# One core, a fused attention, mixture-of-experts and FFN kernel: transposes of the pooled attention's exponentials go behind the next tile's q and k transposes in each step

## The chip, the cores and the metric

The kernel runs on one core of a Trainium2 chip. The metric is the device time of one execution in microseconds (us), lower is better. The engines are named as in the profile: PE (TensorE's matmuls), PEld (its weight loads), DVE (VectorE), ACT (ScalarE), POOL (GpSimd) and SP (SyncE, which here issues nearly all DMAs).

## What is computed

Three layers in a row. The first adds two attentions over q, k, v of shape 4 x 8 x 576 x 64: one over q, k, v pooled by four rows, its output repeated four times, and one local, with a mask of three rows to each side. The second sends each of the 2304 tokens through the one of eight experts that its gate picks. The third is a dense FFN with softplus.

```python
def _attn_ref(q, k, v):                       # factor = 4
    q_d = q.reshape(B, H, Sd, factor, D).mean(axis=3)      # k_d, v_d likewise
    out_d = sm_attn(q_d, k_d, v_d)
    out_up = np.repeat(out_d, factor, axis=2)
    mask = np.abs(pos[:, None] - pos[None, :]) < factor
    scores = np.where(mask, scale * np.matmul(q, k.transpose(0, 1, 3, 2)), -1e9)
    ...
    return out_up + np.matmul(attn, v)

def _moe_ref(x, modality_id, w_gate, modality_bias, w1, w2):
    logits = x @ w_gate + modality_bias[modality_id]
    e_idx = np.argmax(logits, axis=1)
    ...
    out[mask] = gate_w[mask, None] * (np.maximum(x[mask] @ w1[e], 0.0) @ w2[e])

def _moe2_ref(x, w_in, w_out):
    h = x @ w_in
    return (np.maximum(h, 0.0) + np.log1p(np.exp(-np.abs(h)))) @ w_out
```

## The kernel before

The program has two parts. `phase_a` computes the attention and the gate for 18 tiles of 128 tokens (four batches of 4.5 tiles) and writes them to DRAM; `phase_cd` gathers tokens by expert and runs the experts and the FFN. The first part takes roughly the first 205 us of the span, and the change lies in it.

`phase_a` is a software pipeline. A loop counts steps `t`, and each step calls the stages that the string `ORDER` names, from left to right (`ORDER` for steps 0 to 17, `TAIL0` and `TAIL` after that). Stages with nothing to do are skipped. Those that matter here:

- **LG** (`load_vg`, L662 to L666) loads v of a whole batch in four pieces through two buffers, `vg`; DVE adds four rows to one (`vh`, then `vd`). **LV** (`load_v`, L653) loads the v windows.
- **S** (`local_s`, L776 to L781) is tile t's local scores: 16 matmuls on PE into two PSUM banks, the mask added on DVE, the row maximum on DVE. **E** (`local_e`, L786, L787) subtracts it on POOL and exponentiates on ACT.
- **P** (`prep`, L674 to L695) takes a later tile (tile t+5 from step 2 on): four transposes of q and four of k on PE, each group into a bank of its own. ACT copies q out twice (`qbd`, L678), DVE sums four columns of q to one from the same bank (`qd`, L687), ACT copies k (`kT`, L690), and POOL sums k from SBUF (`h2`, `kd`, L693, L695). P ends with the loads of q and k of a tile three further on (L646).
- **DS** (`down_s`, L718 to L723) is one unit of the pooled attention (four heads of a batch): 12 score matmuls into two banks, maximum and subtraction on DVE, exponentials on ACT (`dp`, L723). **DT** (`down_t`, L733, L734) works in the step after on that unit: 12 transposes of the exponentials on PE into three banks, which ACT copies out (`dpt`). **DO** (`down_o`, L745 to L757) multiplies them with `vd`.
- **T** (`local_t`, L796, L797) transposes the local exponentials of tile t-1, **O** (`local_o`, L809 to L813) multiplies them with v. **M** and **G** are the gate, **X** transposes finished tiles for it, **U** and **LU** add the pooled output.

There are eight pooled units, two for each batch. DS runs in the steps in which one is waiting and DT one step later, so DT has work in steps 3, 4, 5, 6, 10, 11, 14 and 15. `PSL` lets P run ahead until the last tile is prepared in step 12. Both stages have work in steps 3, 4, 5, 6, 10 and 11.

All PSUM tiles of `phase_a` come from one tag of eight banks (`b1`). The text of the program doesn't fix the queues: the tile framework's planner puts each engine's instructions in order, with the place in the program as their priority and its own model of time for when they are ready, and it hands a bank to a new tile when a model's reader has released it. A tile that gets a bank waits on the chip for the readers of the tile that had it. Each engine then runs its queue strictly in that order.

```python
    elif what == "DT":
        for x in d_s:
            down_t(*x)
...
    elif what == "P":
        prep_to(PS(t))
```

Of the kernel before, what the change touches and what calls it, by code (L numbers as in the profile page):

```python
# [19 lines left out]
def tile_attention_moe_ffn(  # L20
# [16 lines left out]
    B, H, S, D = q.shape  # L37
# [548 lines left out]
    def phase_a(actx):  # L586
# [520 lines left out]
        LDA, LVA, OL, DN, UN = 2, 1, 1, 1, 2  # L1107
# [1 line left out]
        PSL = (3, 6, 7, 8, 9, 10, 11, 12, 13, 14, 15, 16, 17, 18, 19, 19, 21, 22)  # L1109
        TAIL0 = "DN Z LG LV S DT P E T DS DO U X O U M X M LU XT G G G W"  # L1110
        TAIL = "DN Z LG DS LV S DT P E T O DO LU U X M F G G F F G F W"
        ORDER = "DN Z LG LV S DT P M G T DS X U LU O E DO W"

        def PS(t):
            return PSL[t] if t < len(PSL) else t + 5
# [7 lines left out]
        while q_lu[0] < NTT or q_u or q_x or q_m or q_g:  # L1123
            t += 1
            for what in (ORDER if t < 18 else TAIL0 if t == 18 else TAIL).split():
                step(t, what)
# [262 lines left out]
    with ExitStack() as actx:  # L1389
        phase_a(actx)  # L1390
# [36 lines left out]
```

## Time and profile before

| | us |
|---|---|
| median of 3 runs | 922.46 (918.93 to 923.62) |
| the profiled execution | 925.12 |
| its span, first to last instruction | 923.4 |
| PE busy in the span | 853.3 (92%) |
| DVE busy | 654.7 (71%) |
| ACT busy | 547.1 (59%) |
| POOL busy | 214.8 (23%) |

A busy share is a mean over stages that are bound by different things, so a stage is read by itself: first the busy time and DMA share of a stretch, then the instructions in order of time. A row of the timeline begins with its start and its length in us; behind it, in brackets, stands how long its engine had been idle before it, and what ended that.

### The profile page before, as it was taken

How to read it: one execution, taken by the hardware profiler on the slowest of the kernel's cores; microseconds unless marked ns; L12 is line 12 of the kernel's file. 1: busy time of each engine (PE TensorE's matmuls, PEld its weight loads, DVE VectorE, ACT ScalarE, POOL GpSimd, SP SyncE). 2: the span in 40 equal slices, each digit the busy share in tenths (PEclk: the TensorE clock that was granted, in tenths of full speed). 3: DMA queues.
4: the chain of work that ended last, by engine and by line, in shares of the span. 5: the costliest groups of instructions: out<-in, count | busy, mean ns of one | idle time of the engine just before them, and what ended most of it. 6: DMA issues, size and time to landing. Idle time of an engine off the chain costs nothing. (4 is left out here: it accounts for less than half of the span.)

```text
span 923.4 us, 15325 instructions
## 1 busy us (share of the span) xinstructions
PE 853.3 (92%) x5356; PEld 725.9 (79%) x5356; DVE 654.7 (71%) x1271; ACT 547.1 (59%) x935; POOL 214.8 (23%) x263
## 2 busy tenths in 40 slices
PE   6797899868899999999999999899999999999996
PEld 6687788756777766786687898789899998999984
DVE  6576487678699988976857798656656665666662
ACT  3553564453699777876857677656545555455451
POOL 8322554230243342511001222202000000000001
PEclk9998899799999999999999999999999999999999
DMA  9999785672934599577354333202001001000000
GB/s 164 191 174 195 171 199 126 177 194 94 309 123 138 175 368 332 205 265 252 115 194 147 99 94 109 69 12 65 27 12 35 23 12 34 24 12 12 24 1 34
DMA packets 109112, 115.68 MB, mean 125 GB/s; under 512 B 68448, under 2 KB 83552, under 8 KB 109024
## 3 DMA queue, kind: packets, MB, share of 16 engines
q1 hardware_dynamic: 101072, 98.28, 38.0%
q0 software_dynamic: 4960, 16.28, 5.5%
q8 instruction: 44, 0.72, 0.3%
q10 hardware_dynamic: 2992, 0.04, 0.2%
q14 instruction: 44, 0.36, 0.1%
HBM read 92.93 MB, written 21.65 MB: 124 GB/s over the span
## 5 line engine op out<-in xcount | busy, mean ns | idle before, releaser
L333 DVE TENSOR_TENSOR wl<-raw,wh 128x1024 fp32r<-128x1024 f32 x152 | 187.6, 1256 | 34.8 <-ACT wh L332 31.8
L332 ACT ACTIVATE wh<-raw 128x1024 fp32r<-128x1024 f32 x152 | 159.2, 1064 | 39.8 <-DMA raw<-in_moe_w_dram 16.7
L552 PE MATMUL p<-yh,wh 128*128 128x384 f32 x384 | 131.6, 343 | 11.3 <-DVE e L1239 10.1
L556 PE MATMUL p<-yh,wl 128*128 128x384 f32 x384 | 129.4, 337 | 0.0
L555 PE MATMUL p<-yl,wh 128*128 128x384 f32 x384 | 129.3, 337 | 0.0
L552 PE MATMUL p<-wh,gh 128*128 128x512 f32 x288 | 113.8, 395 | 1.1 <-ACT gh L1244 1.1
L555 PE MATMUL p<-wl,gh 128*128 128x512 f32 x288 | 113.2, 393 | 0.0
L556 PE MATMUL p<-wh,gl 128*128 128x512 f32 x288 | 101.4, 395 | 0.1
L1238 ACT ACTIVATE u<-u 128x384 f32<-128x384 f32 x96 | 50.1, 524 | 80.1 <-DVE e L1237 80.1
L552 PEld LDWEIGHTS p<-yh,wh 128*128 128x128 f32 x384 | 72.1, 188 | 18.7 <-DVE e L1239 14.2
L1245 DVE TENSOR_TENSOR gl<-e,gh 128x384 fp32r<-128x384 f32 x96 | 57.5, 600 | 40.7 <-ACT gh L1244 39.9
L1244 ACT ACTIVATE gh<-e 128x384 fp32r<-128x384 f32 x96 | 50.1, 523 | 45.1 <-DVE e L1240 44.8
L555 PEld LDWEIGHTS p<-yl,wh 128*128 128x128 f32 x384 | 72.2, 188 | 3.0
L1231 ACT ACTIVATE e<-p 128x384 f32<-128x384 f32 x96 | 46.4, 488 | 46.3 <-PE p L556 42.8
L556 PEld LDWEIGHTS p<-yh,wl 128*128 128x128 f32 x384 | 72.1, 188 | 0.3
L1192 POOL DMA_INDIRECT yg<-ys,pos x18 | 19.1, 1060 | 216.4 <-PE p L1209 205.7
L1237 DVE SCALAR_TENSOR_TENSOR e<-u,e 128x384 f32<-128x384 f32 x96 | 55.2, 577 | 13.4 <-ACT u L1234 11.2
L556 PEld LDWEIGHTS p<-wh,gl 128*128 128x128 f32 x288 | 54.0, 188 | 12.9 <-DVE gl L1245 0.8
L552 PEld LDWEIGHTS p<-wh,gh 128*128 128x128 f32 x288 | 54.1, 188 | 10.5 <-ACT gh L1244 1.5
L1240 DVE TENSOR_TENSOR e<-e,u 128x384 f32<-128x384 f32 x96 | 55.3, 579 | 9.0 <-ACT u L1238 1.3
L555 PEld LDWEIGHTS p<-wl,gh 128*128 128x128 f32 x288 | 54.2, 188 | 8.7
L552 PE MATMUL p<-wh,hh 128*128 128x512 f32 x144 | 58.9, 409 | 1.8 <-ACT y L1170 1.5
(256 smaller groups left out, 1800.4 us busy)
## 6 DMA issues: line engine op xcount, KB each, us to landing
raw<-in_moe_w_dram SPq DMA_DIRECT2D x40, 512.0 KB
cv<-in_moe_w_in_dram SPq DMA_DIRECT2D x16, 512.0 KB
cv<-in_moe_w_out_dram SPq DMA_DIRECT2D x16, 512.0 KB
wh<-in_moe_w_dram SPq DMA_DIRECT2D x16, 512.0 KB
wl<-in_moe_w_dram SPq DMA_DIRECT2D x16, 512.0 KB
vw<-in_v_dram SPq DMA_DIRECT2D x36, 144.0 KB
ys<-y SPq DMA_DIRECT2D x20, 256.5 KB
vg<-in_v_dram SPq DMA_DIRECT2D x16, 288.0 KB
```

Of the source, the lines that this page charges most:

```text
L332: ins = (act.activation(out=hi, in_=r, func=ACTF.Copy), dve.tensor_tensor(out=lo, in0=r, in1=f32(hi), op=ALU.subtract))
L333: dve.tensor_tensor(out=lo, in0=r, in1=f32(hi), op=ALU.subtract))
L552: i = pe.matmul(out=ps, lhsT=lh, rhs=rh, start=first, stop=False)
L555: pe.matmul(out=ps, lhsT=lh, rhs=rl, start=False, stop=False)
L556: pe.matmul(out=ps, lhsT=ll, rhs=rh, start=False, stop=last)
L1192: pool.indirect_dma_start(out=y, out_offset=None, in_=ys[0:rows], in_offset=bass.IndirectOffsetOnAxis(ap=pos[:, t:t + 1], axis=0))
L1231: act.activation(out=e, in_=ps, func=ACTF.Abs)
L1237: dve.scalar_tensor_tensor(out=e, in0=u, scalar=-1.0, in1=e, op0=ALU.add, op1=ALU.subtract)
L1238: act.activation(out=u, in_=u, func=ACTF.Ln)
L1240: dve.tensor_tensor(out=e, in0=e, in1=u, op=ALU.add)
L1244: act.activation(out=gh, in_=e, func=ACTF.Copy)
L1245: dve.tensor_tensor(out=gl, in0=e, in1=f32(gh), op=ALU.subtract)
```

## The change

Within a step, P now stands ahead of DT. Nothing is added or removed, and the strings for steps 18 and later stay as they are.

```diff
         TAIL0 = "DN Z LG LV S DT P E T DS DO U X O U M X M LU XT G G G W"
         TAIL = "DN Z LG DS LV S DT P E T O DO LU U X M F G G F F G F W"
-        ORDER = "DN Z LG LV S DT P M G T DS X U LU O E DO W"
+        ORDER = "DN Z LG LV S P DT M G T DS X U LU O E DO W"
```

## Rows read from the trace of the kernel before

**Rows 1.** The page: busy share of PE over the span, and DMA by fortieths.
```profile
PE 853.3 (92%) x5356; PEld 725.9 (79%) x5356; DVE 654.7 (71%) x1271; ACT 547.1 (59%) x935; POOL 214.8 (23%) x263
...
DMA  9999785672934599577354333202001001000000
```

**Rows 2.** Stretches of 5 us: length, each engine's busy time, clock, DMA share, GB/s.
```profile
55.00:60.00 5.00, 3.88 (x24) 3.38 (x23) 3.43 (x13) 3.06 (x6) 0.00 (x0) 0.67 0.91 160
80.00:85.00 5.00, 3.62 (x20) 3.61 (x21) 4.15 (x14) 2.98 (x5) 1.76 (x2) 0.56 0.72 179
85.00:90.00 5.00, 5.00 (x92) 4.36 (x90) 1.45 (x3) 2.84 (x5) 2.85 (x4) 0.76 1.10 230
95.00:100.00 5.00, 2.80 (x15) 2.74 (x15) 3.28 (x6) 0.97 (x3) 3.10 (x4) 0.76 1.17 235
```

**Rows 3.** Timeline of PE: DT (L733) in steps 3 to 6 and 10, P (L674).
```profile
45.68 1.16 PE L733 MATMUL b<-ident,dp 96*72 96x96 f32 x12
46.67 0.60 PE L674 MATMUL b<-ident,q 128*128 128x128 f32 x4
47.11 0.60 PE L674 MATMUL b<-ident,k 128*128 128x128 f32 x4
...
56.29 1.82 PE L733 MATMUL b<-ident,dp 96*72 96x96 f32 x12 [1.03 <-ACT dp L723]
...
67.20 1.18 PE L733 MATMUL b<-ident,dp 96*72 96x96 f32 x12
...
81.38 2.13 PE L733 MATMUL b<-ident,dp 96*72 96x96 f32 x12 [2.14 <-ACT dp L723]
...
119.96 1.16 PE L733 MATMUL b<-ident,dp 96*72 96x96 f32 x12
```

**Rows 4.** Timeline of DVE and ACT: the exponentials that step 6's DT waits for.
```profile
75.89 0.69 DVE L665 TENSOR_TENSOR vh<-vg 72x512 f32<-72x512 f32 x1 [2.54 <-DMA vg<-in_v_dram]
...
79.77 0.60 DVE L721 TENSOR_TENSOR dp<-b,dnm 96x432 f32<-96x432 f32 x1
...
80.40 0.92 ACT L723 ACTIVATE dp<-dp 96x864 f32<-96x864 f32 x1 [5.11 <-DVE dp L721]
```

**Rows 5.** Waits of DVE from 36 to 112 us: total, times, longest.
```profile
DVE vh L665 <- DMA vg<-in_v_dram: 16.0, 13, 2.6
```

**Rows 6.** Timeline of DVE and PE: the next waits of PE, in steps 5 and 7.
```profile
70.40 0.69 DVE L665 TENSOR_TENSOR vh<-vg 72x512 f32<-72x512 f32 x1 [1.26 <-DMA vg<-in_v_dram]
...
71.58 1.07 PE L796 MATMUL b<-ident,s 128*72 128x128 f32 x8 [2.32 <-DVE s L778]
...
95.91 0.87 DVE L665 TENSOR_TENSOR vh<-vg 72x512 f32<-72x512 f32 x1 [2.56 <-DMA vg<-in_v_dram]
...
97.20 0.33 PE L809 MATMUL b<-vw,pT 128*64 128x65 f32 x2 [2.30 <-DVE s L778]
```

**Rows 7.** Timeline of SP: the issue of the q that step 6's P transposes.
```profile
51.01 1.44 SPq L646 DMA_DIRECT2D q<-in_q_dram  x1
```

**Rows 8.** Timeline of ACT and PE: step 3's copies of DT, and their first reader.
```profile
46.21 1.24 ACT L734 ACTIVATE dpt<-b 72x384 f32<-72x384 f32 x3 [0.80 <-PE b L733]
...
50.77 0.27 PE L745 MATMUL b<-vd,dpt 72*64 72x65 f32 x1
```

**Rows 9.** Timeline of PE and DVE: DS (L718) and the q sum (L687), steps 4 and 5.
```profile
60.88 1.63 PE L718 MATMUL b<-kd,qdb 128*96 128x144 f32 x12
...
63.20 0.68 DVE L687 TENSOR_REDUCE qd<-b 128x128 f32<-128x512 f32 x1
...
72.48 1.63 PE L718 MATMUL b<-kd,qdb 128*96 128x144 f32 x12
...
76.50 0.68 DVE L687 TENSOR_REDUCE qd<-b 128x128 f32<-128x512 f32 x1
```

**Rows 10.** Timeline of ACT and PE at the end of the attention.
```profile
203.71 1.06 ACT L332 ACTIVATE wh<-raw 128x1024 fp32r<-128x1024 f32 x1 [5.41 <-DMA raw<-in_moe_w_dram]
...
205.31 0.66 PE L845 MATMUL b<-xT,wg 128*32 128x128 f32 x8 [4.94 <-ACT xT L834]
```

## The prediction

> **What bounds the kernel now.** I read the page first: PE is busy for 92% of the span, and DMA for nine tenths or more only in the first fortieths [rows 1]. Most of the kernel is therefore PE's, but the stretch in which the change lies need not be. The program text says which stretch that is: P and DT both have work only in steps 3, 4, 5, 6, 10 and 11. The timeline of PE shows DT in these steps at 45.68, 56.29, 67.20, 81.38 and 119.96 us [rows 3], and in step 11 in the same way with no wait; so all that is moved lies between 45 and 136 us.
>
> Next I asked for busy time by stretches of 5 us. Between 55 and 100 us the DMA engines are nearly full: shares of 0.91, 0.72, 1.10 and 1.17 in the four stretches shown, at 160 to 235 GB/s [rows 2]. The view of DVE's waits says who suffers: from 36 to 112 us DVE stands 13 times, 16.0 us in all, in front of `vh` (L665) for a piece of v that has not landed [rows 5]. DVE runs in order, so the masks, maxima and subtractions queued behind that instruction stand too. PE then waits for DVE: 2.32 us in step 5 after a piece that came at 70.40, and 2.30 us in step 7 after one that came at 95.91 [rows 6]. Steps 4 to 7 thus go at the pace at which v lands, and PE makes up for what it loses elsewhere in those steps. From about 100 to 155 us PE's waits are short and few.
>
> **The change part by part.** *What is moved.* At full clock DT takes PE from 45.68 to 46.67, 0.99 us, and P takes 0.44 us for q (46.67 to 47.11) and the same again for k, 0.88 us [rows 3]. Where PE doesn't wait ahead of DT, the swap makes P 0.99 us earlier and DT 0.88 us later and saves nothing: steps 3, 10 and 11.
>
> *The waits it can fill.* Ahead of DT, PE waits for the exponentials (ACT L723) 1.03 us in step 4 and 2.14 us in step 6 [rows 3]; in step 5 its weight load waits 0.24 us at 67.19. P needs none of these: its q was issued at 51.01 for use at 83.30 [rows 7], and the other steps have at least 10 us between issue and use. With P in the gap, PE saves at most 0.88 us in step 4, 0.24 in step 5 and 0.88 in step 6: 2.0 us of 3.4 us. The rest of step 6's wait stays, because the exponentials come when they came: DVE stood 2.54 us for a piece of v until 75.89, so the last subtraction started at 79.77 and the exponential at 80.40 [rows 4].
>
> *The clock.* After both long waits the granted clock falls from 2.4 to 1.2 GHz for a while: its mean is 0.67 in 55 to 60 us, and 0.56 and 0.76 in 80 to 90 us [rows 2]. DT then takes 1.82 and 2.13 us instead of 1.16 [rows 3]. In full-clock time this costs (1 - 0.67) x 5 = 1.65 us after step 4 and (0.44 + 0.24) x 5 = 3.4 us after step 6, at most, since PE could not have used all of it. If the first wait goes, its 1.65 us may go too. In step 6 a wait of 2.14 - 0.88 = 1.26 us is left, more than the 1.03 us that was followed by the lower clock in step 4, so I count nothing back there. Bounds of this term: 0 and 5.05 us; I take 1.65, in step 4.
>
> *Where it goes.* Step 4 gains 0.88 + 1.65 = 2.5 us, and step 5 meets its mask addition with 2.32 us more to wait, since DVE frees that only after the piece of v at 70.40 [rows 6]. The 0.2 us left over and the 0.24 us of step 5 end in the wait for step 6's exponentials, which hang on the piece at 75.89. Step 6 gains 0.88 us and meets the wait of step 7, where PE could start at 97.20 only because of the piece at 95.91; that wait grows from 2.30 to 3.2 us. None of these loads waits for P or DT: P's own loads follow P in the program as before and go to buffers that were free ten us and more earlier, and DT issues no DMA, so SP's queue keeps its order. What is late next is therefore v, in both places, and of 3.4 us won some 0 to 1 us reach 100 us. I take 0.5.
>
> *What DT's lateness costs.* Queued behind DT on ACT are the copies of `dpt`. ACT would copy q and k first, 1.2 + 0.6 us. In step 3 `dpt` is done at 46.21 + 1.24 = 47.45 and would be done by about 49.3; its reader, DO, starts at 50.77 [rows 8]. The margins of the other five steps lie between 1.3 and 6 us, so this is hidden; without that cover it would be up to 1.8 us in each of six steps. POOL's two sums of k come up to 1 us earlier and the first reader is steps away: nothing. PE's T stands behind both stages either way: nothing.
>
> *What the trace doesn't show* is the PSUM banks. P now takes its two banks before DT takes its three, so q's bank comes round sooner. It is free only when DVE has done the q sum (L687), and that stands behind `vh` in DVE's queue: it started at 63.20 in step 4 and at 76.50 in step 5, while DS, which takes banks after T, had run at 60.88 and 72.48 [rows 9]. If the planner gives q's bank to the second half of DS in the same step, that half (0.82 us into DS) waits until 63.88 instead of 61.7, or 2.2 us, and until 77.2 instead of 73.3, or 3.9 us; in step 3 the same reading gives 1.0 us. The bounds are 7.1 us of stalls, and a gain of up to 1 us, as the q copies and so the q sum can start earlier and slip ahead of a `vh`. I take 0: the earlier q sum is the nearer case, and PE has slack in steps 5 and 6 for the smaller stalls.
>
> **Sum.** -0.5 us against the profiled execution (925.12 us, span 923.4, 1.7 us around it); that one lies 0.3% above the median of the runs, and I apply the difference to the median: 922.46 - 0.5 = 922.0 us.
>
> **The rivals.** *PE carries it all (faster).* If v lands earlier when PE is earlier, or the planner shifts `vh` to where it doesn't block, the 2.0 us and the 5.05 us of clock all count: 922.5 - 7.1 = 915.4 us; if the waits go whole, 914. Against it: the piece at 95.91 came in a stretch with a DMA share of 1.17 [rows 2, 6]. For it: in 80 to 85 us the share is only 0.72. By the Trainium skill (Perfetto Trace Analysis, Identifying the Most-Contended Engine), DMA is to be judged by its use of HBM and not by how occupied its engines are, and the most-contended engine is the one to improve; by that rule these steps could be PE's and this rival would hold, but DVE's waits for v speak against it here.
>
> *A bank wait takes its place (slower).* The mechanism is the q bank under DS, in steps 4 and 5, at 7.1 us of stalls with step 3, and 1.65 us more for each time that the clock falls after one: 922.5 + 7.1 = 929.6 us, up to 933. It decides if the stalls together exceed the 2.3 us that PE has to spare in step 5 and the 2.1 us in step 6, and if DO, behind DS on PE, comes late for the pooled output of batch 1. For it: eight banks serve some 14 tiles a step, and the q sum is late today. Against it: the q sum is ready earlier after the change. The Trainium skill (Perfetto Trace Analysis, Optimization Strategy) reads a gap that keeps coming back on the busiest engine as a sign of too little PSUM for the next tile, and would look here first; no row of before shows such a gap between T and DS.
>
> *It doesn't do what it says.* The planner could leave DT ahead of P where its model has the exponentials ready: 922.5 us. The queue of PE follows the program order of the stages in all six steps, so this is unlikely.
>
> *The rest of the plan shifts.* A new plan can move queue positions far behind the change. At 203.71 ACT stands 5.41 us in front of a weight piece and PE waits 4.94 us for what is queued behind it [rows 10]; such a wait can go or another one come. That is about 5 us to either side, and the reason why I keep both sides nearly even.
>
> **How the numbers follow.** Forecast (absorbed) 0.47, faster rival 0.22, slower rival 0.20, not done 0.05, plan shifts beyond the bound 0.03 to either side. A measurement of this kernel tells about 0.5% (4.6 us) from no change, so faster is 0.22 + 0.03 = 0.25, slower 0.20 + 0.03 = 0.23, and the same 0.52. The range takes in both rivals' nearer ends with a little room: 914.5 to 930.5 us. The forecast's own range is 919 to 925.
>
> **What would show it.** Right: PE runs P straight after S in steps 4 and 6, DT still waits for ACT L723 in step 6 by about 1.3 us, the clock no longer falls near 56 us, and PE's waits for DVE in steps 5 and 7 are longer by what was won, so that the tile of step 7 leaves PE at the same time. Wrong to the fast side: those waits are no longer, and stages after 100 us lie several us earlier. Wrong to the slow side: a gap in PE ahead of DS or O that ends with DVE L687. If the attention ends where it did but the total differs by more than 5 us, the plan of the later stages has changed, and my view of the six steps says nothing on it.

## The result: 0.86% slower, lost a hundred microseconds behind the change

| | before | after |
|---|---|---|
| median of 14 runs each, same chip | 920.39 (915.15 to 926.36) | 929.01 (922.86 to 934.56) |
| ratio after / before | | 1.0086, 95% interval 1.0058 to 1.0114 |
| span of the profiled execution | 923.4 | 931.0 |

The change costs 8.6 us. The time lies in the range I gave, but the forecast was no change. The page of after, beside [rows 1], shows nothing of a cause: PE is as busy a share of the span as before, with 4 us more busy time.

```profile
span 931.0 us, 15336 instructions
...
PE 857.3 (92%) x5356; PEld 727.8 (78%) x5356; DVE 659.2 (71%) x1271; ACT 547.6 (59%) x935; POOL 216.8 (23%) x263
```

So I cut the span into stretches. The first view is again the 5-us stretches, to be held against [rows 2] (length, busy time of PE, PEld, DVE, ACT and POOL, granted clock, DMA share, GB/s), of after:

```profile
55.00:60.00 5.00, 3.63 (x34) 3.12 (x34) 3.32 (x13) 4.18 (x8) 0.00 (x0) 1.00 0.92 163
70.00:75.00 5.00, 3.00 (x17) 2.57 (x15) 3.54 (x8) 2.42 (x6) 1.48 (x2) 0.73 0.91 158
80.00:85.00 5.00, 3.79 (x38) 3.52 (x37) 4.45 (x15) 4.32 (x8) 1.88 (x2) 1.00 0.86 191
85.00:90.00 5.00, 3.71 (x87) 3.51 (x88) 1.37 (x2) 1.17 (x2) 2.80 (x4) 1.00 1.08 237
```

The clock no longer falls in steps 4 and 6: 1.00 where it had been 0.67, 0.56 and 0.76. It falls in step 5 instead: 0.73 in 70 to 75 us, where before had 1.00. The timeline of PE in after shows the swap and what came with it, beside [rows 3] and [rows 6]:

```profile
55.62 0.60 PE L674 MATMUL b<-ident,q 128*128 128x128 f32 x4
56.05 0.60 PE L674 MATMUL b<-ident,k 128*128 128x128 f32 x4
56.49 0.49 PE L733 MATMUL b<-ident,dp 96*72 96x96 f32 x4
58.06 0.50 PE L733 MATMUL b<-ident,dp 96*72 96x96 f32 x4 [1.07 <-DVE drs L749]
58.86 0.50 PE L733 MATMUL b<-ident,dp 96*72 96x96 f32 x4 [0.30 <-DVE drs L750]
...
63.32 0.85 PE L745 MATMUL b<-vd,dpt 72*64 72x65 f32 x21 [1.15 <-DVE qd L687]
...
69.78 0.50 PE L733 MATMUL b<-ident,dp 96*72 96x96 f32 x4 [0.44 <-DVE x L813]
72.28 1.92 PE L796 MATMUL b<-ident,s 128*72 128x128 f32 x8 [2.00 <-DVE s L778]
...
81.75 1.16 PE L733 MATMUL b<-ident,dp 96*72 96x96 f32 x12
...
96.42 0.48 PE L809 MATMUL b<-vw,pT 128*64 128x65 f32 x2 [2.04 <-DVE s L778]
```

P stands in front of DT, and DT's waits for the exponentials (ACT L723) are gone in both steps. In their place DT waits for PSUM banks, 1.07, 0.30 and 0.44 us, until DVE has read what was in them. The view puts the first two down to L749 and L750, but L750 reads no bank; what fits all three is O's L813, which reads O's result and ends at 57.91, 58.71 and 69.63, each time 0.15 us ahead of DT's start. In step 4 these L813 stand behind a `vh` that came at 56.89 after 1.65 us of waiting for a piece of v. DO (L745) waits 1.15 us in step 4 for the q sum (DVE L687). The wait of step 5 is now at 72.28, that of step 7 at 96.42, each within 0.8 us of its place before. At the end of the attention, beside [rows 10]:

```profile
203.97 1.06 ACT L332 ACTIVATE wh<-raw 128x1024 fp32r<-128x1024 f32 x1 [4.60 <-DMA raw<-in_moe_w_dram]
...
205.56 0.66 PE L845 MATMUL b<-xT,wg 128*32 128x128 f32 x8 [4.51 <-ACT xT L834]
```

The gate's matmul stands at 205.56 us instead of 205.31. The stage that was changed ends 0.25 us later; that is next to nothing of 8.6.

The loss lies in the expert stage. Its marks are ACT's copies of the finished slots (`y`, L1170), one in each slot of some 14 us. In after they start 1.4 us earlier than before at 292.4 and at 305.9 us, 3.1 us later at 320.1, 6.3 later at 346.7, 9.6 later at 377.4 and 9.4 to 10.1 later from 391.3 to the last slot. The profiled span is 7.6 us longer, so some 2 us come back behind the experts. In the stretches view, from the attention (45 to 205 us) on, of before and then of after:

```profile
45.00:205.00 160.00, 136.69 (x1799) 124.08 (x1793) 111.79 (x335) 79.12 (x153) 62.25 (x74) 0.91 0.78 175
...
225.00:305.00 80.00, 75.24 (x360) 60.96 (x359) 69.43 (x93) 65.61 (x85) 26.62 (x13) 1.00 0.58 189
305.00:391.00 86.00, 82.11 (x371) 57.92 (x370) 76.48 (x97) 65.09 (x87) 33.79 (x20) 0.98 0.77 272
```

```profile
45.00:205.00 160.00, 135.37 (x1785) 123.02 (x1784) 111.08 (x334) 79.08 (x153) 62.96 (x74) 0.92 0.75 174
...
225.00:305.00 80.00, 78.05 (x371) 63.19 (x370) 70.60 (x93) 66.57 (x87) 25.02 (x13) 0.99 0.56 186
305.00:391.00 86.00, 77.92 (x326) 53.19 (x327) 70.49 (x87) 56.60 (x78) 31.73 (x19) 0.93 0.74 262
```

From 305 to 391 us PE has 4.2 us less busy time and a granted clock of 0.93 instead of 0.98, which is 0.05 x 86 = 4.3 us at full clock: 8.5 us together. Which waits these are is told by the view of waits from 295 to 395 us (total, times, longest), for PE in before:

```profile
PE p L556 <- DVE hl L527: 2.0, 1, 2.0
PE p L552 <- ACT y L1170: 1.1, 2, 0.6
PE p L556 <- DVE xl L527: 0.6, 1, 0.6
```

and for PE, then DVE, in after:

```profile
PE p L556 <- DVE xl L527: 5.7, 2, 3.8
PE p L552 <- ACT y L1170: 2.8, 2, 2.3
...
DVE cz L213 <- DMA wf<-cz: 5.0, 3, 2.3
...
DVE cy L209 <- DMA cv<-in_moe_w_in_dram: 2.7, 1, 2.7
```

L527 makes the second half of the gathered tokens, `xl`, for the matmuls of the next slot; L1170 is the copy of `y`. What stands in front of the two longest of these waits, on DVE and ACT, is the **weight conversion**: during the expert slots sixteen pieces of the FFN's weights are loaded (`cv`, L188 and L191 on SP), taken apart on ACT (`cm`, L206) and DVE (`cy`, L209; `cz`, L213), added on POOL (L215) and stored (`wf`, L217). One slot of the two kernels, first before (ACT, then DVE):

```profile
372.71 0.60 ACT L526 ACTIVATE xh<-p 128x512 fp32r<-128x512 f32 x1
...
374.26 0.43 DVE L209 TENSOR_SCALAR cy<-cv 128x512 int32<-128x512 int32 x1 [1.63 <-DMA cv<-in_moe_w_in_dram]
374.61 1.22 DVE L333 TENSOR_TENSOR wl<-raw,wh 128x1024 fp32r<-128x1024 f32 x1
375.74 0.68 DVE L527 TENSOR_TENSOR xl<-p,xh 128x512 fp32r<-128x512 f32 x1
```

and the same slot in after (ACT, DVE, PE):

```profile
378.00 0.60 ACT L526 ACTIVATE xh<-p 128x512 fp32r<-128x512 f32 x1
...
378.38 0.69 DVE L213 SCALAR_TENSOR_TENSOR cz<-cv,cy 128x512 int32<-128x512 int32 x1 [2.32 <-DMA wf<-cz]
378.99 1.22 DVE L333 TENSOR_TENSOR wl<-raw,wh 128x1024 fp32r<-128x1024 f32 x1
382.95 0.43 DVE L209 TENSOR_SCALAR cy<-cv 128x512 int32<-128x512 int32 x1 [2.74 <-DMA cv<-in_moe_w_in_dram]
383.30 1.22 DVE L333 TENSOR_TENSOR wl<-raw,wh 128x1024 fp32r<-128x1024 f32 x1
384.43 0.68 DVE L213 SCALAR_TENSOR_TENSOR cz<-cv,cy 128x512 int32<-128x512 int32 x1
385.03 1.22 DVE L333 TENSOR_TENSOR wl<-raw,wh 128x1024 fp32r<-128x1024 f32 x1
386.17 0.69 DVE L527 TENSOR_TENSOR xl<-p,xh 128x512 fp32r<-128x512 f32 x1
...
382.67 0.40 PE L555 MATMUL p<-wl,xh 128*128 128x512 f32 x1
386.91 1.22 PE L556 MATMUL p<-wh,xl 128*128 128x512 f32 x2 [3.84 <-DVE xl L527]
387.93 0.63 PE L552 MATMUL p<-wh,xh 128*128 128x512 f32 x1
```

In before `xl` starts 3.0 us after `xh` has started on ACT. In after it starts 8.2 us after. Three instructions of the conversion stand between them in DVE's queue instead of one, and three `wl` (L333, half of an expert weight, 1.22 us each) instead of one. The first `cz` had waited 2.32 us for a store to give its buffer back, but nearly all of that lay ahead of `xh`: it starts only 0.4 us behind it. The `cy` in the middle waits 2.74 us for its load, and PE, which needs only `xl`, waits 3.84 us. Its matmuls then take 0.63 us, where the one ahead of the wait took 0.40. Something like it happens on ACT at 322.10 (timeline of after, POOL, ACT and PE): on POOL the addition for `cz` stands behind a gather that runs from 314.90 to 320.77, ACT's `cm` waits for that addition, and the copies of `hh` and `y` wait behind `cm`.

```profile
314.90 5.87 POOL L521 DMA_INDIRECT xg<-xs,gidx  x1 [10.06 <-DVE cz L213]
...
322.10 0.67 ACT L206 ACTIVATE cm<-cv 128x512 int32<-128x512 uint32 x1 [5.81 <-POOL cz L215]
...
323.89 0.50 PE L552 MATMUL p<-wh,hh 128*128 128x512 f32 x1 [2.27 <-ACT y L1170]
```

The third wait, 1.81 us, is of another kind: between 302.49 us and `xl` three `wl` stand on DVE and nothing of the conversion (DVE and PE).

```profile
302.49 4.57 DVE L333 TENSOR_TENSOR wl<-raw,wh 128x1024 fp32r<-128x1024 f32 x3
...
307.71 1.18 PE L556 MATMUL p<-wh,xl 128*128 128x512 f32 x2 [1.81 <-DVE xl L527]
```

No line of the expert stage was changed. In the two traces the instructions stand in the same order on every queue from 225 us on, except in a stretch that in before runs from 270 to 385 us. In it the planner put the conversion elsewhere: loads and stores behind other weight loads on SP, `cm` at other places on ACT, `cy` and `cz` on DVE, and the addition for `cz` on POOL. Some `wh` and `wl`, the halves of the expert weights, moved with them.

### The profile page after: what moved, and what is told of

The parts are those of the page before. It is cut to its first block, busy times and chain, and to the rows that moved or that the text cites. A ratio compares the mean times of both kernels' runs of the same rounds, so it can differ in the third digit from the quotient of the medians.

```text
span 931.0 us, 15336 instructions
## 1 busy us (share of the span) xinstructions
PE 857.3 (92%) x5356; PEld 727.8 (78%) x5356; DVE 659.2 (71%) x1271; ACT 547.6 (59%) x935; POOL 216.8 (23%) x263
## 5 line engine op out<-in xcount | busy, mean ns | idle before, releaser
L333 DVE TENSOR_TENSOR wl<-raw,wh 128x1024 fp32r<-128x1024 f32 x152 | 189.5, 1268 | 33.0 <-ACT wh L332 31.8
L1237 DVE SCALAR_TENSOR_TENSOR e<-u,e 128x384 f32<-128x384 f32 x96 | 55.2, 577 | 13.5 <-ACT u L1234 11.2
L556 PE MATMUL p<-wh,xl 128*128 128x512 f32 x136 | 55.8, 423 | 7.1 <-DVE xl L527 7.1
```

The source lines that it names most:

```text
L333: dve.tensor_tensor(out=lo, in0=r, in1=f32(hi), op=ALU.subtract))
L556: pe.matmul(out=ps, lhsT=ll, rhs=rh, start=False, stop=last)
L1237: dve.scalar_tensor_tensor(out=e, in0=u, scalar=-1.0, in1=e, op0=ALU.add, op1=ALU.subtract)
```

## The experiments

**Theory A**: the loss is this other plan of the expert stage, which the swap brings about through the planner. **Theory B**: the swapped steps lose, through DT's new waits for banks. A swap in steps 3, 4, 5 and 11 together leaves the queues from 225 us on in before's order, while a swap in step 6 alone or in step 10 alone puts them in after's; the traces of the three runs show it. So steps can be swapped with either plan behind them. The edit of the first three runs, with other steps in the tuple:

```diff
-        ORDER = "DN Z LG LV S DT P M G T DS X U LU O E DO W"
+        ORDER = "DN Z LG LV S DT P M G T DS X U LU O E DO W"; SWAP = "DN Z LG LV S P DT M G T DS X U LU O E DO W"; SWAPPED = (3, 4, 5, 11)
...
-            for what in (ORDER if t < 18 else TAIL0 if t == 18 else TAIL).split():
+            for what in (SWAP if t in SWAPPED else ORDER if t < 18 else TAIL0 if t == 18 else TAIL).split():
```

**Steps 3, 4, 5 and 11 swapped.**

> P ahead of DT in steps 3, 4, 5 and 11 alone; steps 6 and 10 keep the old order. The queues of this program stand after 225 us in the order of the kernel before. Theory A (the loss comes from the expert stage, whose queues the planner filled in another order): the loss is gone, 919 to 921.5 us, ratio 0.997 to 1.002. Theory B (the swapped steps themselves lose, by DT's new bank waits in steps 4 and 5, 1.07 + 0.30 + 0.44 us in the trace of after, and by what follows from them): most of the loss stays, 924 to 929 us, ratio 1.004 to 1.009.

Measured: 923.6 us, ratio 0.9989 (0.9958 to 1.0020). The loss is gone, although steps 4 and 5 are swapped; DT's waits for banks are there in step 4 (0.52 and 0.31 us), and so is DO's 1.15 us for the q sum. The 923.6 us lie above the 921.5 that I gave, but the kernel before ran at 923.89 beside it. A holds, B falls for these steps.

**Step 10 swapped** (`SWAPPED = (10,)`), a step in which PE had no wait to fill.

> P ahead of DT in step 10 alone, where PE waits for neither of them in the kernel before. The queues of this program stand after 225 us in the order of the kernel after. Theory A: the whole loss is here, 927 to 931 us, ratio 1.006 to 1.012. Theory B: no loss, 919.5 to 921.5 us, ratio 0.998 to 1.002.

Measured: 936.83 us, ratio 1.0130 (1.0092 to 1.0167): the loss, and more than A's upper end. **Step 6 swapped** (`SWAPPED = (6,)`):

> P ahead of DT in step 6 alone, where PE waits 2.14 us ahead of DT in the kernel before. The queues after 225 us again stand in the order of the kernel after. Theory A: 927 to 931 us, ratio 1.006 to 1.012. Theory B, whose bank waits are in steps 4 and 5: 919 to 921.5 us, ratio 0.997 to 1.002, or less if the wait that is filled pays.

Measured: 931.47 us, ratio 1.0083 (1.0053 to 1.0114). Both runs with after's plan lose, and PE's waits for `xl` from 295 to 395 us are 8.2 and 9.0 us, against 0.6 in the run of steps 3, 4, 5 and 11. But the plan and steps 6 and 10 go together here, so B is not yet excluded for those two.

**The whole swap, the conversion held in program order.**

```diff
 def conv_load():
-            if c >= CD:
+            if True:
                 tc.keep_in_program_order(i)
...
 def conv_work():
-            if c >= CD:
+            if True:
                 tc.keep_in_program_order(i1)
```

The second edit stands twice, for `cm` on ACT and for `cy` on DVE.

> The kernel after, with the loads, the first ACT copy and the first DVE instruction of the weight conversion in the expert stage held in program order, so that the planner can't move them about. Theory A: the expert stage is another than in both kernels and the time can be anything from 915 to 935 us, but PE's waits of 2 to 4 us for DVE near 323 and 387 us, which stand behind the conversion in DVE's queue, change. Theory B: still 927 to 931 us, since nothing before 225 us is touched.

Measured: 928.15 us, ratio 1.0041 (1.0016 to 1.0066). By the ratio, and with nothing touched that runs before the expert stage, half the loss is gone, but the run doesn't decide: A allowed any time from 915 to 935 us, and 928.15 lies in B's 927 to 931 too. In it PE's waits for `xl` from 295 to 395 us fall from 5.7 to 0.9 us, though one of 3.2 us for `hl` comes in their place. Part of the gain is given back from 391 us on, where these pins put the rest of the conversion: the mark at 391.3 lies 6.6 us earlier than before, the last slot's 4.1 us later.

**The plan apart from the swap.** To part the plan from steps 6 and 10, something else has to move it. In step 17, where no pooled unit is left, calling G ahead of M does that: with all six steps swapped it brings before's later queues back, and with none swapped it brings after's, but for a few of SP's instructions ahead of 245 us.

```diff
-            for what in (ORDER if t < 18 else TAIL0 if t == 18 else TAIL).split():
+            for what in (ORDER.replace("M G", "G M") if t == 17 else ORDER if t < 18 else TAIL0 if t == 18 else TAIL).split():
```

On the kernel after:

> All six steps swapped as in the kernel after, and in step 17 the stage G (one step of each gate) called ahead of M (the gate's matmuls). In the program as built, the queues from the expert stage's fifth slot on are then those of the kernel before, but for one instruction of PE; the attention's are those of the kernel after up to step 17. Theory A (the loss is the later plan): the loss is gone although every swapped step is in, ratio 0.996 to 1.004, 920 to 928 us, and PE's waits for the halves of x at L527 between 295 and 395 us fall from 5.7 us to under 1.5 us. Theory B (the swapped steps 6 and 10 themselves lose, which the runs of 6 alone and 10 alone did not exclude): the loss stays, ratio 1.006 to 1.012.

Measured: 924.46 us, ratio 1.0009 (0.9975 to 1.0043). On the kernel before:

> No step swapped; only in step 17 G is called ahead of M, as in the run beside it. In the program as built the later queues are then those of the kernel after, but for one instruction of PE, four of DVE and ten of SP. Theory A: the loss appears although no transposes were moved, ratio 1.005 to 1.013, 926 to 936 us, with the waits for L527 of 5 us or more between 295 and 395 us; the difference to the run beside it is +5 to +11 us. Theory B: no loss, ratio 0.997 to 1.003, and the difference to the run beside it is -5 us or more to the other side. What the gate's moved step costs by itself is in both runs and drops out of their difference.

Measured: 937.53 us, ratio 1.0136 (1.0095 to 1.0178). The difference of 13.1 us has A's sign; it is 2 us more than A's upper end, and 5.9 of it are there at 292.4 us already (the table below). PE's waits from 295 to 395 us follow the plan and not the swap, in the run with all six steps swapped:

```profile
PE p L556 <- DVE hl L527: 2.1, 1, 2.1
PE p L556 <- DVE xl L527: 1.3, 2, 0.7
PE p L552 <- ACT y L1170: 1.1, 2, 0.6
```

and in the run with none swapped, where 4.9 us for `xl` are just under the 5 that A had:

```profile
PE p L556 <- DVE xl L527: 4.9, 2, 3.1
PE p L552 <- ACT y L1170: 3.0, 2, 2.4
```

B has fallen: the loss appears with no transposes moved, and is absent with all of them moved. Set side by side, with the start of the copies of `y` in each profile against that in before's (us):

| swapped | later queues as in | ratio | `y` at 292.4 | `y` at 391.3 | lost between the two |
|---|---|---|---|---|---|
| 3, 4, 5, 11 | before | 0.9989 | +3.0 | +1.0 | -2.0 |
| all six, G first in 17 | before | 1.0009 | -0.5 | +0.6 | 1.1 |
| all six (after) | after | 1.0086 | -1.4 | +9.4 | 10.8 |
| 6 | after | 1.0083 | -1.4 | +11.4 | 12.8 |
| 10 | after | 1.0130 | +2.2 | +13.3 | 11.1 |
| none, G first in 17 | after | 1.0136 | +5.4 | +14.8 | 9.4 |

The offsets are from one profile of each kernel. With after's plan 9.4 to 12.8 us are lost in these hundred microseconds, with before's -2.0 to 1.1. The two largest ratios belong to profiles that are already 3.6 and 6.8 us later than after at 292.4, ahead of the place where the plans differ; that part is not the plan's, and its cause was not looked for.

**A third buffer for the converted weights**, in after. Is it the wait of `cz` for its store that makes this plan slow?

```diff
-                z = cvp[-1].tile([128, DM], I32, tag="cz", name="cz")
+                z = cvp[-1].tile([128, DM], I32, tag="cz", name="cz", bufs=3)
```

> Kernel after with three buffers in place of two for the converted weights cz; in the program as built the later plan stays the one of the kernel after but for some twenty instructions. Theory A1: what makes this plan slow is that DVE, in front of the second half of x (L527), stands waiting for a store of cz to free its buffer (L213, 5.0 us in 295 to 395 us) and so passes on the loads of cv behind it; with a third buffer that wait falls under 1 us, the longest wait of PE for L527 falls from 3.8 to under 2 us, and half the loss or more is back: ratio 1.000 to 1.005. Theory A2: the waits on stores only cover others (the loads of cv on SP behind the expert weights' loads, POOL's gathers in front of cz), so that L209 or L206 wait for cv instead and PE waits as long: ratio 1.006 to 1.011.

Measured: 931.32 us, ratio 1.0083 (1.0049 to 1.0117). No wait for a store is left among DVE's from 295 to 395 us, but the wait for the load behind it has grown from 2.7 us, and PE waits nearly as long as in after (DVE, then PE):

```profile
DVE cy L209 <- DMA cv<-in_moe_w_in_dram: 5.4, 1, 5.4
...
PE p L556 <- DVE xl L527: 5.3, 2, 3.5
```

A1 falls, as the 0.4 us above already suggest: the wait for the store only covered the wait for the load behind it, and DVE still reaches `cy`, ahead of `xl`, before that load has landed; `cy` starts at 382.54 us instead of 382.95.

**No swap, the conversion held in program order**: the edit of the pinned run on the kernel before.

> Kernel before with the conversion's loads, its copies on ACT and its first step on DVE held in program order: the partner of the pinned run with the swap, whose later queues differ from these in some sixty instructions of PE and DVE and four of SP. Theory A: with nearly the same later plan the swap costs next to nothing, so this run comes out at the pinned swap's time, ratio 1.001 to 1.007 (924 to 930 us). Theory B: the swap itself costs, and this run is 5 us or more faster than the pinned swap, ratio 0.993 to 0.999.

Measured: 931.51 us, ratio 1.0076 (1.0046 to 1.0106), just above A's range. It is not faster than the pinned run with the swap, as B would have it, but 0.35% slower, and the two intervals overlap. The pins by themselves cost time on the kernel before, and are no remedy.

**No conversion in the expert stage**, with and without the swap. If the plans differ only by where they put the conversion, they must cost the same without it. Left out are the loads, the work on ACT, DVE and POOL, and the stores of these sixteen pieces; the FFN reads as many bytes of w1 in their place, so its output is no longer the FFN's.

```diff
             c, j = conv.pop(0)
+            if c < CD: return
             t = cvp[-1].tile([128, DM, 2], I32, tag="cv", name="cv", bufs=2)
...
-            x = sp.dma_start(out=t, in_=wf[s])
+            x = sp.dma_start(out=t, in_=w1r[128 * s:128 * s + 128])
```

> Kernel after without the conversion of the first half of the FFN weights in the expert stage (its loads, its work on ACT, DVE and POOL and its stores are left out; the FFN reads the same number of bytes from w1 instead, so its values are others). Theory A, narrowed to its place (the later plan costs because conversion steps stand in front of the halves of x and the copies of y on DVE and ACT): without them PE waits less than 1.5 us for L527 between 295 and 395 us, the time is at or under that of the kernel before, 905 to 922 us, and the run beside it, without the swap, is within 3 us. Theory C (the later plan costs by the places of the expert weights' loads and of the gathers, whatever the conversion does): this run stays 5 us or more above the one beside it.

> Kernel before without the conversion of the first half of the FFN weights in the expert stage, as in the run beside it (the FFN's values are others). Theory A, narrowed: 905 to 922 us, within 3 us of the run with the swap; what it lies under the kernel before is what the conversion costs in before's plan, and by the waits there (PE's 3.7 us for L527 and L1170 between 295 and 395 us, and the lower clock after them) that is 2 to 10 us. Theory C: 5 us or more under the run with the swap.

Measured: 912.92 us with the swap, ratio 0.9868 (0.9833 to 0.9902), and 912.20 us without, ratio 0.9852 (0.9816 to 0.9889). They are 0.7 us apart, where before and after are 8.6 apart. The stretch from 295 to 395 us, first with the swap, then without:

```profile
295.00:395.00 100.00, 100.00 (x480) 75.54 (x479) 73.22 (x90) 74.69 (x97) 10.99 (x10) 1.00 0.56 196
```

```profile
295.00:395.00 100.00, 100.00 (x478) 75.41 (x477) 76.27 (x91) 76.07 (x97) 11.05 (x10) 1.00 0.51 177
```

PE is busy without a gap, at full clock, in both. Theory C's forecast of 5 us or more between them fails, and that of the narrowed A holds. The pair has a limit: without the conversion the two programs hardly differ in this stretch (a handful of instructions on each queue between 270 and 395 us). So it shows that the plans' difference and the loss both go with the conversion and its transfers, and not that after's places of the other work cost nothing; the wait of 1.81 us behind `wl` is such a cost. For the two longer waits the trace of after names the conversion itself: its load on DVE, its addition on POOL. From 295 to 395 us it puts no wait of PE, and none of ACT or DVE at `wh` or `wl`, down to a load of expert weights. One number of mine was too small: leaving the conversion out brings 924.91 x (1 - 0.9852) = 13.7 us in before's plan, not 2 to 10. In after's plan it brings 1.0086 - 0.9868 = 2.2%, some 20 us.

**What stays open.** Why the planner's choice turns on these steps is not known; only that it does, and with which edits. Nor is the loss divided between the conversion's instructions, its transfers and the places of `wh` and `wl`. What the swap does to the attention by itself is too small to be told: with equal or nearly equal plans behind it the swap reads as -0.35% (both pinned), +0.16% (no conversion), -0.11% (steps 3, 4, 5 and 11 beside before) and +0.09% (all six, G first in step 17, beside before), each less than its uncertainty. And no run here shows a version faster than before with the whole computation in it; keeping the conversion's instructions out of the places in front of `xl` and `y` until their loads are in was not tried.

## Why the prediction was wrong

The step that failed is the rival **"The rest of the plan shifts"**: sized at about 5 us to either side by a wait at 203.71 us and, beyond that, given a chance of 0.03 to either side, with nothing in the sum. The shift measured 10.8 us, between 305 and 391 us. The steps on the attention held in the main. That 929.0 us lies in the range, and near the 929.6 of the slower rival, is luck: that rival's bank waits are not what made the kernel slower. With before's plan behind it the swap reads -0.11% and +0.09%, so the forecast of -0.5 us for the six steps is neither confirmed nor refuted; by the two intervals it is at most some 4 us to either side.

- *The waits P can fill*: right. DT's waits for ACT L723 are gone in steps 4 and 6. For step 6 I had left 1.26 us of wait; none is left, since the exponential begins at 80.12, 0.3 us earlier than in [rows 4], and PE leaves S only at 80.88, 1.6 us later than before (81.38 - 2.14 = 79.24). Nearly all of that delay comes from step 5, where T starts 0.7 us later and takes 0.85 us longer, and I hadn't foreseen it: most of step 6's wait went because PE was late, not because P filled it.
- *The clock*: right in step 4, where 55 to 60 us is at 1.00 as taken. In step 6 I counted nothing back, because a wait longer than step 4's 1.03 us would remain; it didn't remain, and 80 to 90 us is at 1.00 too. At these two places the term was its upper bound, 5.05 us, and not 1.65; but most of it was lost elsewhere, as in 70 to 75 us. Over the whole attention, 45 to 205 us, the lower clock took 14.4 us of full-clock time before and 13.5 us after: 1 us is left.
- *Where it goes*: right as to the sum, half right as to the way. The matmul that waits in step 7 starts 0.8 us earlier and the gate's matmul at the end 0.25 us later, so nearly nothing reached the end. But the waits behind the pieces of v didn't lengthen by what was won: 2.00 and 2.04 us, against 2.32 and 2.30 in [rows 6]. Part of the gain went into other waits first. From 45 to 136 us PE's waits sum to 12.8 us, against 10.8 before: the banks, 1.41 us ahead of T in step 3 (0.42 before), and in step 6 1.22 and 1.29 us of O for T's copies on ACT (L797), of which I had listed none.
- *PSUM banks*: I looked at the wrong stage. DS never waited for the q sum (L687); DO did, 1.15 us in step 4, which is close to the sign that I had named for the slow side. And DT's own second and third bank weren't free until DVE had read O's result. I had taken 0, with bounds of -1 to +7.1; together it measured 1.07 + 0.30 + 0.44 + 1.15 = 3.0 us. Nearly nothing of it reached the end of the attention, and in the run of steps 3, 4, 5 and 11, where 2.0 us of these waits stand, there is no loss; so the rival built on banks is not what made this kernel slower.
- *The rest of the plan shifts*: here it failed, twice. I sized it by one wait that I happened to see next to the change, 5.41 and 4.94 us in [rows 10]. Those moved to 4.60 and 4.51 us, by less than 1 us. The shift came a hundred microseconds later, in a stage whose rows I hadn't read, and was 10.8 us there. And I gave it 0.03 on either side beyond the bound, although I had written that the planner orders all queues by a model of time: under such a planner a local move can be a new draw of every queue behind it, and the rows from 295 to 395 us would have shown how much hung on it there. In before's own profile PE already waits 3.7 us for `xl`, `hl` and `y`, with DMA at a share of 0.77.

My last sentence under "What would show it" named this case, an attention that ends where it did and a total more than 5 us off; I should have made it a case with a price and not a disclaimer.

## What to carry to other kernels

Where a planner orders the queues, compare the built queues over the whole program before you argue from the stretch that was edited: if they differ elsewhere, the stages in which they differ belong in the sum, each with the waits that an in-order engine would take on if a load behind it were late. To part an edit from the plan that it brings about, look for a second, unrelated edit that moves the plan the other way, and run all four. Work that is put into another stage's gaps (the conversion here) costs what stands behind it on the same queues, and its price can be measured by leaving it out.

## What the runs showed of the hardware

Waits of PE of similar length didn't have the same consequence for its clock, which goes between two levels, 2.4 and 1.2 GHz (1.00 and 0.50 of the granted clock). In step 4 before, 1.03 us of wait ahead of DT were followed by a mean of 0.67 in 55 to 60 us; in after, 1.07 us inside DT, with P's transposes just ahead, left it at 1.00. In step 5 it is the other way round: before, a wait of 2.32 us left the clock at 1.00 in 70 to 75 us, and T's eight transposes behind it took 1.07 us [rows 6]; in after 2.00 us were followed by 0.73, and the same eight took 1.92 us. So the length of the last wait alone doesn't tell whether the clock falls.

In the expert stage, from 295 to 395 us, each fall came with a wait: 2.04 us at 384.39 in before; 1.81 us at 307.71, 2.27 us at 323.89 and 3.84 us at 386.91 in after. Matmuls of 0.63 us instead of 0.40 followed each. Waits of up to 0.59 us there were followed by none, and without the conversion PE ran these 100 us without a gap at 1.00.
